# Row sums that go through DRAM in three units instead of one, with outputs scaled a pair later, and a third buffer for weight quarters

## The chip, the cores and the metric

The kernel runs on one core of one Trainium2 chip. The metric is device time in microseconds of one execution of the whole program. Three executions of the kernel before gave a median of 539.22 us (536.98 to 544.5). The engines are PE (TensorE, matrix products and transposes), DVE (VectorE), ACT (ScalarE), POOL (GpSimd) and SP (SyncE), whose queue issues nearly all DMAs of this program, strictly in the order in which they are written.

## The reference

Attention with a learned position bias for 4 batches, 8 heads, 576 positions and head size 64, followed by a gated feed-forward block (512 to 1024 to 512) with a convolution over three positions:

```python
scores = scale * q @ k.T + bias            # bias: a small network on the distance |i - j|
attn   = exp(scores - max) ; attn = attn / (sum(attn) + 1e-09)
x      = attn @ v                          # (4, 576, 512), heads side by side
h      = relu(x @ w_in)
out    = (h * sigmoid(conv3(h))) @ w_out
```

What matters for this change is the division by the sums of the rows. The kernel leaves it out of the attention matrix, computes the output of the pair unscaled, and multiplies it by the inverse sums afterwards. And the feed-forward weights, in float32, are split into two parts that TensorE multiplies at its faster float32 rate; this is done a quarter of 128 rows at a time, in small steps beside the attention.

## The kernel before

**Pairs and units.** Attention goes through 16 pairs (two heads, one batch), numbered n = 0 to 15, four batches for each pair of heads. A pair has five units, in the order `units = [1, 2, 3, 4, 0]`; `ui` is the place in this list, 0 to 4. I write (n, ui). In the loop over units (`for u, (n, t) in enumerate(flat)`), a unit does the scores of the unit two ahead (L341 on PE; L348 on DVE adds the bias and takes the minimum of the negated scores), the exponentials of the unit one ahead (L362, ACT), and its own transposes (L397, PE, copied out by ACT L88 and DVE L91) and products with v (L441, PE). The order on every engine is the order of the Python program: nothing is reordered, so an instruction that waits holds up all that stands behind it on its engine.

**The sums.** At the end of (n, 0) `invert(n - 1)` takes the reciprocals of the sums of pair n-1 (L461, L462, DVE). In (n, 2) they are transposed with the other blocks (L404) and copied to `rt` (L91). Then, still in (n, 2), `normalise(n - 1)` has SP store `rt` to DRAM in three small DMAs (`r_d<-rt`, L472 to L474) and read it back spread over 64 partitions each in two DMAs (`rb<-r_d`, L477, 144 KB each). The read waits on SP until the stores have landed. In (n, 4) `apply_norm(n - 1, rb)` has POOL multiply the output of the pair by `rb` (L483, 128 x 576). `rb` has one buffer.

**The weight quarters.** There are 28. Every second unit SP is asked for one (`raw_w`, L118, 256 KB); three units later its steps begin, in the two units that follow, one step per half unit: ACT L96 and DVE L97 (`w<-raw_w`), DVE L99, DVE L103, and in the fourth step POOL's split (L130, L131) of `w` into `wi` or `wo`. The tile `w` has one place for all quarters, so L97 of the next quarter, at the start of the next unit, waits for POOL's split of this one. `raw_w` has two buffers, and the ask for quarter j+2 stands in the unit in which L96 and L97 free the buffer of quarter j.

**SP's other work.** In (n, 2) it loads q and k of pair n+2 (L149, L150, four DMAs) and v of pair n+1 (L164 to L167, four DMAs). When the next pair of heads is near (from (n, 3) of pairs 2, 6 and 10 to (n, 2) of the pair behind) it also loads the bias rows of the next pair of heads, two DMAs per unit (L175, 288 KB each; L177).

After the loop come the last pair's sums and the feed-forward block (L504, L699 to L729).

Of the kernel before, what the change touches and what calls it, by code (L numbers as in the profile page):

```python
# [9 lines left out]
F32 = mybir.dt.float32  # L10
F32R = mybir.dt.float32r
I32 = mybir.dt.int32
# [7 lines left out]
def attention_ffn_kernel(  # L20
# [11 lines left out]
    nc = tc.nc  # L32
    B, S, DM = out.shape
# [5 lines left out]
    P = 128  # L39
# [19 lines left out]
    def pool(stack, name, bufs, **kw):  # L59
        return stack.enter_context(tc.tile_pool(name=name, bufs=bufs, reuse_waits="tile", **kw))  # L60
# [10 lines left out]
    e_p = pool(ctx, "e", 2)  # L71
    woe_p = pool(ctx, "woe", 1)
# [11 lines left out]
    NSEQ = len(seq)  # L84
# [32 lines left out]
    def load_w(raw, src):  # L117
        nc.sync.dma_start(raw.rearrange("p n t -> p (n t)"), src.bitcast(I32))  # L118
# [14 lines left out]
    with tc.manual_schedule():  # L133
# [9 lines left out]
        def load(n):  # L143
            p, b = seq[n]
            qks[n] = t = q_p.tile([P, KO + S], F32, name="qk")
            keys = qk[b, p, :, KO:].rearrange("d (h a s) -> d a h s", h=2, a=2)
            for a in range(2):
                rows = slice(D * a, D * a + D)
                nc.sync.dma_start(t[rows, 0:KO], qk[b, p, :, 0:KO])  # L149
                nc.sync.dma_start(halves(t[rows, KO:]), keys[:, a])  # L150
# [147 lines left out]
        rb_p = pool(att, "rb", 1)  # L298
# [9 lines left out]
        xb = {0: x0}  # L308
# [18 lines left out]
        def scores(n, t, h):  # L327
            p, b = seq[n]
            qt, bt = qks[n], biast[p, t]
            if h == 0:  # L330
                if n not in sms:
                    sms[n] = sm_p.tile([P, 9], F32, name="sm")
                nms[n, t] = sm_p.tile([P, 2], F32, name="nm")
                new_sp(n, t)
            ps = psS.tile([P, 2, 512], F32, name="s")
            ops = [(h, h * QW + P * t)] if t else [(1, QW), (0, 0)]

            for i, (hh, qo) in enumerate(ops):
                for a in range(2):
                    rows = slice(D * a, D * a + D)  # L340
                    nc.tensor.matmul(  # L341
                        ps[:, a, 0:HS],
                        qt[rows, qo:qo + P],
                        qt[rows, KO + hh * HS:KO + hh * HS + HS],
                        start=(i == 0),
                        stop=(i == len(ops) - 1),
                    )
            nc.vector.tensor_tensor_reduce(  # L348
                out=halves(spt[n, t][0][:, h]),
                in0=ps[:, :, 0:HS],  # L350
                in1=halves(bt[:, h]),
                op0=ALU.add,
                op1=ALU.min,
                scale=-scale,
                scalar=3.0e38,
                accum_out=nms[n, t][:, h:h + 1],
            )

        def expo(n, t, h):
            sp, nm = spt[n, t][0], nms[n, t]  # L360
            col = 4 * h + t - 1 if t else 8
            exps[n, t, h] = nc.scalar.activation(  # L362
                sp[:, h], sp[:, h], AF.Exp, bias=nm[:, h:h + 1], scale=-1.0,
                accum_out=sms[n][:, col:col + 1],
            )
# [6 lines left out]
        def ends_group(n, t):  # L372
            return t in (0, 2, 4) or n == 0 and t == 3
# [93 lines left out]
            rts[n] = r_p.tile([9, P], F32, name="rt")  # L467
            dve(rts[n], ps[0:9, 0:P])

        def normalise(n):  # L470
            rt = rts.pop(n)
            nc.sync.dma_start(r_d[n, 0, TL:].rearrange("(t x) -> t x", x=P), rt[0:4])  # L472
            nc.sync.dma_start(r_d[n, 1, TL:].rearrange("(t x) -> t x", x=P), rt[4:8])
            nc.sync.dma_start(r_d[n:n + 1, :, 0:TL], rt[8:9].rearrange("o (h x) -> o h x", h=2))  # L474
            rb = rb_p.tile([P, S], F32, name="rb")
            for h in range(2):
                nc.sync.dma_start(rb[D * h:D * h + D], r_d[n, h:h + 1, :].to_broadcast([D, S]))  # L477
            return rb

        def apply_norm(n, rb):  # L480
            p, b = seq[n]
            assert waiting[n] == 0
            nc.gpsimd.tensor_mul(xb[b][:, p], xb[b][:, p], rb)  # L483


        xss = {}
# [10 lines left out]
        def ffn_in(b, f):  # L497
            ps = psS.tile([P, 2, 512], F32, name="s")
            cs = slice(f * P, f * P + P)
            i = 0  # L500
            for c in range(KC):
                for pw, px in ((0, 0), (0, 1), (1, 0)):
                    for a in range(2):
                        nc.tensor.matmul(  # L504
                            ps[:, a, 0:HS],
                            wi[c][:, pw, cs],
                            xss[b, c][:, px, a * HS:(a + 1) * HS],
                            start=(i == 0),
                            stop=(i == 3 * KC - 1),
                        )  # L510
                    i += 1
            if (b, f) in ((0, 0), (0, 1)):
                h = e_p.tile([P, S], F32, name="h")
            else:
                h = g_p[0].tile([P, S], F32, name="h", tag="g")
            nc.scalar.activation(halves(h), ps[:, :, 0:HS], AF.Relu)  # L516
            return h
# [35 lines left out]
        def heads(t):  # L553
            return (0, 1) if t else (0,)
# [48 lines left out]
                for h in heads(flat[0][1]):  # L603
                    expo(*flat[0], h)
        pv_share = (2, 5, 3, 2, 3)
        rb = None
        hs_ff = {}
        raw_w = {}
        job_steps = iter(())
# [3 lines left out]
        for u, (n, t) in enumerate(flat):  # L613
            p, b = seq[n]
            ui = units.index(t)
            for h in range(2):
                if u + 2 < NU:
                    if h in heads(flat[u + 2][1]):
                        scores(*flat[u + 2], h)
                if u + 1 < NU and h in heads(flat[u + 1][1]):  # L620
                    expo(*flat[u + 1], h)
            transposes(n, t, 0)
            next(job_steps, None)

            parts = len(fill) if u < 5 else pv_share[ui]
            while fill and parts > 0:
                fill.popleft()()
                parts -= 1
            if t:
                transposes(n, t, 1, n - 1 if ui == 2 and n else None)  # L630
            next(job_steps, None)
            del spt[n, t]
            if u + 2 >= NU:
                f = u + 2 - NU
                hs_ff[0, f] = ffn_in(0, f)
            if u == 1 or n and ui == 2 and n + 2 < NSEQ:
                load(2 if u == 1 else n + 2)
            if u in conv_weights:
                conv_weights[u]()

            for at, do in ((u - 8, "load"), (u - 11, "split")):
                job = at // 2
                if at % 2 == 0 or not 0 <= job < 4 * KC + 2 * FE:
                    continue
                if job < 4 * KC:
                    src, dst = w_in[job // 4 * P:job // 4 * P + P], wi[job // 4]
                else:
                    src, dst = w_out[(job - 4 * KC) // 2 * P:(job - 4 * KC) // 2 * P + P], wo[(job - 4 * KC) // 2]
                cs = slice(job % 4 * 256, job % 4 * 256 + 256) if job < 4 * KC else slice(job % 2 * 256, job % 2 * 256 + 256)
                if do == "load":  # L650
                    raw_w[job] = e_p.tile([P, 256, 2], I32, name="raw_w", tag="h")
                    load_w(raw_w[job], src[:, cs])
                else:
                    job_steps = split_w_steps(e_p, dst[:, :, cs], raw_w.pop(job), ("cv", "cv"))
            if u + 2 < NU:
                n2, t2 = flat[u + 2]
                p2, b2 = seq[n2]
                if b2 == B - 1 and p2 + 1 < NP:
                    load_bias(p2 + 1, t2)
            if ui == (0 if n > 1 else 1) and n > 0:  # L660
                invert(n - 1)
            if ui == (2 if n > 1 else 3) and 1 <= n and n + 1 < NSEQ:
                load_v(n + 1)
            if ui == 2 and n > 0:
                rb = normalise(n - 1)
            if ends_group(n, t):
                fill.extend(pv_parts(n, group(n, t)))
            if ui == 4 and n > 0:
                apply_norm(n - 1, rb)
            if n == NSEQ - 2 and ui > 1:  # L670
                x_parts(0, ui - 2)
            if n == NSEQ - 1 and ui == 0:
                x_parts(0, 3)
            if n == NSEQ - 1 and ui in (1, 2):
                load_wo(FE - 1 + ui)
# [1 line left out]
            fill.popleft()()  # L677
        invert(NSEQ - 1)
        turn_sums(NSEQ - 1)
        apply_norm(NSEQ - 1, normalise(NSEQ - 1))  # L680
        att.close()


# [194 lines left out]
```

## Time and profile before

| | |
|---|---|
| median of three executions | 539.22 us (536.98 to 544.5) |
| the profiled execution | 545.77 us, of which the trace spans 543.9 us |
| PE busy | 503.7 us (93%) |
| DVE busy | 389.1 us (72%) |
| ACT busy | 313.5 us (58%) |
| POOL busy | 103.4 us (19%) |
| mean granted clock of TensorE | 0.971 |

How to read it: the attention loop lies between about 66 and 325 us of the span, the bias network before it and the feed-forward block behind it. PE is the engine that is nearly always busy, so time is lost where PE stands, and where its granted clock (1.00 is 2.4 GHz, 0.50 is 1.2 GHz) is low. In a row of a timeline the first number is the start in us from the span's start, the second the duration, and the brackets at the end give how long the engine stood idle just before, and what ended that wait.

### The profile page before, as it was taken

The page shows a single profiled execution, that of the slowest core. Times are in us where ns is not written, and L with a number is a line of the kernel's source. Part 1 is how long each engine was busy: PE and PEld are TensorE (multiplying, and loading weights), DVE is VectorE, ACT ScalarE, POOL GpSimd, SP SyncE. Part 2 cuts the span into 40 slices and gives each one's busy share as a digit, 9 for nine tenths or more (in the row PEclk, how much of TensorE's full clock was granted, in tenths as well). Part 3 has the DMA queues.
Part 4 walks back from the last instruction along what each step waited for, and adds up shares of the span by engine and source line. Part 5 has one row for each costly group of instructions (what it writes and reads, how often), then busy time and mean ns, then how long its engine had stood idle before and what let it go on. Part 6 is the DMA issues. An engine that isn't in the chain of part 4 may idle for free.

```text
span 543.9 us, 11908 instructions
## 1 busy us (share of the span) xinstructions
PE 503.7 (93%) x4542; PEld 389.3 (72%) x4542; DVE 389.1 (72%) x919; ACT 313.5 (58%) x813; POOL 103.4 (19%) x123
## 2 busy tenths in 40 slices
PE   5999989995899799898989999989999999999995
PEld 3332467774577577575767768978998899889985
DVE  6999677683788488586777763996499349928910
ACT  6888778784588477576767773662262235215510
POOL 1000001021222212232122541453007000700000
PEclk9999999999799899899999999979999999999998
DMA  6789545596557766557776211000200200020001
GB/s 164 265 245 342 205 114 129 126 281 165 141 126 184 233 185 160 137 145 217 190 190 158 66 57 62 23 0 0 78 2 1 78 20 0 1 78 0 2 39 60
DMA packets 32707, 63.50 MB, mean 117 GB/s; under 512 B 5490, under 2 KB 11146, under 8 KB 32650
## 3 DMA queue, kind: packets, MB, share of 16 engines
q1 hardware_dynamic: 32506, 62.66, 40.2%
q8 instruction: 36, 0.59, 0.5%
q14 instruction: 21, 0.17, 0.1%
q10 hardware_dynamic: 144, 0.08, 0.1%
HBM read 46.74 MB, written 15.98 MB: 115 GB/s over the span
## 4 chain that ended last, share of the span: by engine, by line
PE 58%; DMA 12%; DVE 5%; ACT 5%; POOL 3%; SPq 2%; issue 1%; POOLq 0%; DVEq 0%
PE s L504 16%; PE tp L729 14%; PE o L441 10%; PE s L341 7%; PE tp L397 6%; PE o L729 4%; DMA rb<-r_d 4%; DMA qk<-in_qk_dram 4%; DMA r_d<-rt 3%; ACT sp L362 2%; POOL x L483 2%; DVE cv L704 1%; ACT pt L88 1%; DMA bt<-bias_d 1%; ACT x L88 1%
## 5 line engine op out<-in xcount | busy, mean ns | idle before, releaser
L348 DVE CUSTOM_DVE_ANT_0 sp<-s,bt 128x576 f32<-128x576 f32 x144 | 103.6, 750 | 22.2 <-PE s L341 11.4
L362 ACT ACTIVATE sp<-sp,nm 128x576 f32<-128x576 f32 x144 | 109.9, 766 | 1.7 <-DVE nm L348 1.6
L441 PE MATMUL o<-pt,vt 128*64 128x256 f32 (+2 forms) x940 | 100.7, 344 | 10.1 <-DVE pt L91 7.7
L504 PE MATMUL s<-xs,wi 128*128 128x288 f32 x768 | 106.6, 301 | 2.7 <-ACT h L516 2.7
L504 PEld LDWEIGHTS s<-xs,wi 128*128 128x128 f32 x768 | 105.4, 193 | 3.7 <-ACT h L516 2.9
L397 PE MATMUL tp<-identr,sr 64*128 64x64 f32 x1312 | 97.0, 264 | 11.5 <-DVE rt L91 7.6
L397 PEld LDWEIGHTS tp<-identr,sr 64*128 64x128 f32 x1312 | 75.0, 138 | 44.5 <-issue 20.5
L341 PE MATMUL s<-qk 64*128 64x288 f32 x640 | 103.2, 437 | 0.7 <-DVE nm L348 0.6
L88 ACT ACTIVATE pt<-tp 128x256 f32<-128x256 f32 (+2 forms) x160 | 59.6, 383 | 63.1 <-PE tp L397 34.2
L91 DVE COPY pt<-tp 128x256 f32<-128x256 f32 (+2 forms) x160 | 66.5, 425 | 29.6 <-PE tp L397 15.7
L441 PEld LDWEIGHTS o<-pt,vt 128*64 128x64 f32 x940 | 53.2, 139 | 30.5 <-DVE pt L91 9.6
L341 PEld LDWEIGHTS s<-qk 64*128 64x128 f32 x640 | 59.7, 193 | 18.2 <-DVE pt L91 4.6
L729 PE MATMUL tp<-wo,g 128*128 128x512 f32 x288 | 70.2, 390 | 0.0
L704 DVE SCALAR_TENSOR_TENSOR cv<-h,cw,cv 128x575 f32<-128x575 f32 x64 | 60.8, 950 | 2.4 <-ACT cv L699 0.4
L483 POOL TENSOR_TENSOR x<-x,rb 128x576 f32<-128x576 f32 x16 | 22.8, 1425 | 206.5 <-ACT pt L88 101.6
L729 PEld LDWEIGHTS tp<-wo,g 128*128 128x128 f32 x288 | 54.0, 188 | 11.0
L260 PE MATMUL s<-y,pars 128*32 128x512 f32 (+8 forms) x352 | 46.4, 509 | 4.2 <-ACT st L286 2.0
L243 DVE TENSOR_SCALAR y<-tl,inv,nb 128x512 f32<-128x512 f32 (+8 forms) x116 | 49.9, 504 | 0.0
L516 ACT ACTIVATE h<-s 128x576 f32<-128x576 f32 x32 | 20.8, 650 | 48.9 <-PE s L504 48.8
L710 ACT ACTIVATE cv<-cv 128x576 f32<-128x576 f32 x32 | 21.8, 682 | 29.5 <-DVE cv L704 29.5
L260 PEld LDWEIGHTS s<-y,pars 128*32 128x32 f32 x352 | 16.1, 115 | 28.0 <-DVE y L243 13.3
L130 POOL TENSOR_SCALAR xs<-x 128x576 fp32r<-128x576 f32 x16 | 15.1, 942 | 83.5 <-PE s L504 83.5
(66 smaller groups left out, 454.5 us busy)
## 6 DMA issues: line engine op xcount, KB each, us to landing
qk<-in_qk_dram SPq DMA_DIRECT2D x32, 320.0 KB
bt<-bias_d SPq DMA_DIRECT2D x32, 288.0 KB
bias_d<-st SPq DMA_DIRECT2D x14, 607.0 KB
qk<-in_qk_dram SPq DMA_DIRECT2D x32, 144.0 KB
rb<-r_d SPq DMA_DIRECT2D x32, 144.0 KB
out_dram<-o SPq DMA_DIRECT2D x17, 256.0 KB
raw_w<-in_moe_w_in_dram SPq DMA_DIRECT2D x16, 256.0 KB
vt<-in_v_dram SPq DMA_DIRECT2D x16, 224.0 KB
```

The lines of the kernel that those rows point to most:

```text
L88: nc.scalar.activation(o, i, AF.Copy)
L91: nc.vector.tensor_copy(o, i)
L243: nc.vector.tensor_scalar(y, dist[:, 0:n], inv[:, ig:ig + 1], nb1, op0=ALU.mult, op1=ALU.max)
L260: nc.tensor.matmul(ps[32 * j:32 * j + 32, a // 512 if n > 512 else blk % 2, 0:min(n - a, 512)], w2b, ys[j][:, a:min(n, a + 512)], start=Tr ...
L341: nc.tensor.matmul(ps[:, a, 0:HS], qt[rows, qo:qo + P], qt[rows, KO + hh * HS:KO + hh * HS + HS], start=(i == 0), stop=(i == len(ops) - 1),)
L348: nc.vector.tensor_tensor_reduce(out=halves(spt[n, t][0][:, h]), in0=ps[:, :, 0:HS], in1=halves(bt[:, h]), op0=ALU.add, op1=ALU.min, scale ...
L362: exps[n, t, h] = nc.scalar.activation(sp[:, h], sp[:, h], AF.Exp, bias=nm[:, h:h + 1], scale=-1.0, accum_out=sms[n][:, col:col + 1],)
L397: tr = nc.tensor.transpose(ps[a][0:cols, bk - 4 * h].bitcast(F32R), spf[ra, j:j + cols], identr[ra, ra])
L441: nc.tensor.matmul(po[hs, oc], vt[:, slot, :], rhs, start=(c == 0), stop=(c == 4))
L504: nc.tensor.matmul(ps[:, a, 0:HS], wi[c][:, pw, cs], xss[b, c][:, px, a * HS:(a + 1) * HS], start=(i == 0), stop=(i == 3 * KC - 1),)
L704: nc.vector.scalar_tensor_tensor(out=cv[:, o:o + S - 1], in0=h[:, i:i + S - 1], scalar=cw[:, f, kk:kk + 1], in1=cv[:, o:o + S - 1], op0=AL ...
L729: nc.tensor.matmul(ps, lhs(f, gi), wo[f][:, wj, cs], start=(f == 0 and i == 0), stop=(f == FC - 1 and i == 2),)
```

## The change

The one function `normalise` becomes two. `store_sums(n - 1)` stands in (n, 3), a unit later than before; `spread_sums(n - 1)`, the read back, stands in (n, 4), two units later; `apply_norm(n - 2)` stands in (n, 1), which for the same pair is two units after its old place. `load_v` of (n, 2) thereby stands ahead of the stores, as it did before, but the read back has moved behind what stands in (n, 3). For the last pairs the calls follow after the loop. The weight quarters are asked for in the unit before (u - 7 in place of u - 8 in a test that takes every second unit, so an ask moves from odd u to the even u ahead of it), and every third of them takes its buffer from the pool `woe`, so there are three.

```diff
-        def normalise(n):
+        def store_sums(n):
             rt = rts.pop(n)
             nc.sync.dma_start(r_d[n, 0, TL:].rearrange("(t x) -> t x", x=P), rt[0:4])
             nc.sync.dma_start(r_d[n, 1, TL:].rearrange("(t x) -> t x", x=P), rt[4:8])
             nc.sync.dma_start(r_d[n:n + 1, :, 0:TL], rt[8:9].rearrange("o (h x) -> o h x", h=2))
-            rb = rb_p.tile([P, S], F32, name="rb")
+
+        def spread_sums(n):
+            rbs[n] = rb = rb_p.tile([P, S], F32, name="rb")
             for h in range(2):
                 nc.sync.dma_start(rb[D * h:D * h + D], r_d[n, h:h + 1, :].to_broadcast([D, S]))
-            return rb
 
-        def apply_norm(n, rb):
+        rbs = {}
+
+        def apply_norm(n):
             p, b = seq[n]
             assert waiting[n] == 0
-            nc.gpsimd.tensor_mul(xb[b][:, p], xb[b][:, p], rb)
+            nc.gpsimd.tensor_mul(xb[b][:, p], xb[b][:, p], rbs.pop(n))
...
-            for at, do in ((u - 8, "load"), (u - 11, "split")):
+            for at, do in ((u - 7, "load"), (u - 11, "split")):
...
-                    raw_w[job] = e_p.tile([P, 256, 2], I32, name="raw_w", tag="h")
+                    raw_w[job] = (e_p if job % 3 else woe_p).tile([P, 256, 2], I32, name="raw_w", tag="h")
                     load_w(raw_w[job], src[:, cs])
...
-            if ui == 2 and n > 0:
-                rb = normalise(n - 1)
+            if ui == 3 and n > 0:
+                store_sums(n - 1)
+            if ui == 4 and n > 0:
+                spread_sums(n - 1)
             if ends_group(n, t):
                 fill.extend(pv_parts(n, group(n, t)))
-            if ui == 4 and n > 0:
-                apply_norm(n - 1, rb)
+
+            if ui == 1 and n > 1:
+                apply_norm(n - 2)
...
         invert(NSEQ - 1)
         turn_sums(NSEQ - 1)
-        apply_norm(NSEQ - 1, normalise(NSEQ - 1))
+        apply_norm(NSEQ - 2)
+        store_sums(NSEQ - 1)
+        spread_sums(NSEQ - 1)
+        apply_norm(NSEQ - 1)
```

SP's queue in pair 6, from the last load of v to the bias rows. `raw_w` is a weight quarter, `r_d<-rt` a store of sums, `rb<-r_d` their read back, `bt` bias rows. Before:

```order
L167 DMA vt_107<-in_v_dram 64x64
L472 DMA r_d<-rt 4x128
L473 DMA r_d<-rt 4x128
L474 DMA r_d<-rt 2x1x64
L477 DMA rb<-r_d 64x576 x2
L175 DMA bt<-bias_d 128x576 x2
L118 DMA raw_w<-in_moe_w_in_dram 128x512
L175 DMA bt<-bias_d 128x576 x4
```

With the change:

```order
L167 DMA vt_107<-in_v_dram 64x64
L118 DMA raw_w<-in_moe_w_in_dram 128x512
L175 DMA bt<-bias_d 128x576 x2
L472 DMA r_d<-rt 4x128
L473 DMA r_d<-rt 4x128
L474 DMA r_d<-rt 2x1x64
L175 DMA bt<-bias_d 128x576 x2
L479 DMA rb<-r_d 64x576 x2
L118 DMA raw_w<-in_moe_w_in_dram 128x512
L175 DMA bt<-bias_d 128x576 x4
```

The read back, which stood right behind the stores, now has two bias DMAs between it and them, and a quarter and two more bias DMAs ahead of the stores.

POOL's queue from the multiply for pair 4 to the multiply for pair 5 (L483 before, L486 with the change), with the splits of weight quarters (L130, L131) behind them. Before:

```order
L483 TENSOR_TENSOR x_121<-x_121,rb 128x576
L130 TENSOR_SCALAR wi_758<-w 128x256
L131 TENSOR_TENSOR wi_758<-w,wi_758 128x256
L130 TENSOR_SCALAR wi_759<-w 128x256
L131 TENSOR_TENSOR wi_759<-w,wi_759 128x256
L483 TENSOR_TENSOR x_945<-x_945,rb 128x576
```

With the change:

```order
L486 TENSOR_TENSOR x_121<-x_121,rb 128x576
L130 TENSOR_SCALAR wi_759<-w 128x256
L131 TENSOR_TENSOR wi_759<-w,wi_759 128x256
L130 TENSOR_SCALAR wi_759<-w 128x256
L131 TENSOR_TENSOR wi_759<-w,wi_759 128x256
L486 TENSOR_TENSOR x_945<-x_945,rb 128x576
```

The multiply for pair 4 stood ahead of the last split into `wi_758`, and now stands behind it: one quarter, which is two units, further on.

## Rows read from the trace of the kernel before

**Rows 1.** Waits, 66 to 325 us: engine, line, releaser; total us, times, longest.

```profile
POOL x L483 <- DMA rb<-r_d: 80.0, 10, 16.0
DVE w L97 <- POOL wi L131: 17.7, 5, 7.7
DVE w L97 <- POOL wo L131: 8.4, 3, 4.0
PE o L441 <- DVE pt L91: 7.7, 3, 2.9
PE tp L397 <- DVE rt L91: 7.6, 3, 5.4
```

**Rows 2.** The same view for SP's queue, 66 to 325 us.

```profile
SPq L477 <- DMA r_d<-rt: 27.1, 17, 2.8
SPq L118 <- DVE w L97: 25.5, 7, 6.1
```

**Rows 3.** Timeline 178 to 187 us, one wait of PE followed back.

```profile
178.15 1.11 SPq L477 DMA_DIRECT2D rb<-r_d  x2
...
182.76 1.40 POOL L483 TENSOR_TENSOR x<-x,rb 128x576 f32<-128x576 f32 x1 [8.54 <-DMA rb<-r_d]
...
184.61 0.73 POOL L131 TENSOR_TENSOR wi<-w,wi 128x256 fp32r<-128x256 f32 x1
...
185.37 0.29 DVE L97 TENSOR_SCALAR w<-raw_w 128x256 int32<-128x256 int32 x1 [4.46 <-POOL wi L131]
...
186.12 1.12 PE L441 MATMUL o<-pt,vt 128*64 128x256 f32 x4 [2.89 <-DVE pt L91]
```

**Rows 4.** Stretch 186 to 189: busy PE, PEld, DVE, ACT, POOL; clock, DMA share, GB/s.

```profile
186.00:189.00 3.00, 2.88 (x13) 1.36 (x14) 1.74 (x6) 0.00 (x0) 1.09 (x2) 0.50 1.03 335
```

**Rows 5.** Timeline of DVE: the reciprocals at the ends of (n, 0).

```profile
124.10 0.22 DVE L462 RECIPROCAL rr<-rr 128x9 f32<-128x9 f32 x1
149.60 0.22 DVE L462 RECIPROCAL rr<-rr 128x9 f32<-128x9 f32 x1
164.32 0.22 DVE L462 RECIPROCAL rr<-rr 128x9 f32<-128x9 f32 x1
179.02 0.22 DVE L462 RECIPROCAL rr<-rr 128x9 f32<-128x9 f32 x1
200.55 0.21 DVE L462 RECIPROCAL rr<-rr 128x9 f32<-128x9 f32 x1
235.26 0.21 DVE L462 RECIPROCAL rr<-rr 128x9 f32<-128x9 f32 x1
250.09 0.21 DVE L462 RECIPROCAL rr<-rr 128x9 f32<-128x9 f32 x1
286.46 0.22 DVE L462 RECIPROCAL rr<-rr 128x9 f32<-128x9 f32 x1
302.52 0.22 DVE L462 RECIPROCAL rr<-rr 128x9 f32<-128x9 f32 x1
```

**Rows 6.** Timeline of DVE, a small wait for POOL's split.

```profile
289.99 0.29 DVE L97 TENSOR_SCALAR w<-raw_w 128x256 int32<-128x256 int32 x1 [1.62 <-POOL wo L131]
```

**Rows 7.** Timeline 104 to 138 us, SP and PE around pairs 2 to 4.

```profile
104.53 0.62 SPq L474 DMA_DIRECT2D r_d<-rt  x1
107.38 1.12 SPq L477 DMA_DIRECT2D rb<-r_d  x2
129.05 1.61 PE L441 MATMUL o<-pt,vt 128*64 128x256 f32 x12 [1.65 <-DMA vt<-in_v_dram]
137.69 0.69 PE L397 MATMUL tp<-identr,sr 64*128 64x64 f32 x7 [5.35 <-DVE rt L91]
```

**Rows 8.** Timeline 230 to 238 us, a multiply beside DVE's L103.

```profile
231.05 0.41 DVE L103 SCALAR_TENSOR_TENSOR w<-u,w 128x256 int32<-128x256 int32 x1
...
236.48 1.41 POOL L483 TENSOR_TENSOR x<-x,rb 128x576 f32<-128x576 f32 x1 [3.71 <-ACT sr L323]
237.03 1.15 DVE L103 SCALAR_TENSOR_TENSOR w<-u,w 128x256 int32<-128x256 int32 x1
```

More of the change, by code (lines that the diff above doesn't have):

```diff
@@ L605, in attention_ffn_kernel @@
         pv_share = (2, 5, 3, 2, 3)
-        rb = None
         hs_ff = {}
```

## The prediction

> **What bounds the kernel now.** The page gives PE busy for 93% of the span, so I look for the places where PE stands, and for what ends these waits. First the list of waits in the attention loop [rows 1]. PE's large waits there are for copies by DVE: 7.7 us in three times and 7.6 us in three times. DVE itself waits, in its line L97 (the first step of a weight quarter), for POOL's split of the quarter before: 17.7 us in five times and 8.4 us in three times, 26.1 us together, the longest 7.7 us. And POOL waits for the sums read back from DRAM: 80.0 us in ten times. POOL has time to wait; DVE, which stands behind it, has not.
>
> Then the timeline of one case, read from its end [rows 3]. PE gets its copy at 186.12 after 2.89 us of idleness; DVE's L97, which stands ahead of that copy, came at 185.37 after 4.46 us; POOL's split began its last part at 184.61, straight behind the multiply, which came at 182.76 because `rb` landed only then. SP had asked for `rb` at 178.15. So a transfer that PE needs for nothing stops PE, through two queues that keep their order. It costs more than the wait: in the 3 us behind it PE's granted clock is 0.50, which is 1.2 GHz [rows 4]. PE had stood for 2.89 us before.
>
> What one such case costs in all, clock included, is best read from a mark that comes once in every pair, the reciprocals [rows 5]. From 149.60 to 164.32 to 179.02 nothing of the kind costs time, and a pair takes 14.72 and 14.70 us, so 14.71 us, or 2.94 us a unit. From 179.02 to 200.55 (the case above) it takes 21.53 us: 6.82 us more, of which 2.89 are the wait and some 3.9 the low clock. From 124.10 to 302.52 lie ten pairs in 178.42 us. Ten plain ones would be 147.1 us. So 31.3 us of the loop are lost to waits of this kind and their clock.
>
> **The change, part by part.** It adds and removes no instruction: 16 multiplies, 48 stores, 32 reads and 28 quarters stay. It moves them.
>
> *The multiply two units on.* L97 of DVE must not wait for a multiply that waits for `rb`. The multiply moves two units, hence the L97 that stands behind it too: `rb` may land 2 x 2.94 = 5.88 us later than before. The eight waits of L97 are the measure of how late it was. The next longest after the one of 7.7 us is that of the case above, 4.46 us [rows 3]; seven go, with at least 1.4 us to spare, if `rb` does not come later. The eighth was 7.7 us [rows 1] and would keep 1.8 us.
>
> *The read back, later on SP.* What the ask is now behind must be subtracted. An ask takes SP about 0.56 us (1.12 us for two [rows 7]). In a plain pair one or two quarters come ahead of the ask in place of standing behind it, 0.6 to 1.1 us; on the other side SP spends 27.1 us in 17 times waiting at the read for the stores to land, 1.6 us each [rows 2], and the quarter between stores and read, where there is one, fills part of that. I take 0.5 us net: the spare stays near 0.9 us. In pairs 6 and 10 four bias DMAs also come ahead. Their asks are 4 x 0.56 = 2.2 us, mostly inside SP's wait for the stores; their 1152 KB at the 335 GB/s of [rows 4] are 3.4 us of transfer. At 178.15 the stores' landing had left the transfer engines little to do, so I charge about half of it: 1.3 to 1.7 us against the 1.4 us to spare. L97 may wait there for up to about a microsecond. Wait sizes have a price: 1.62 us [rows 6] stand in a pair of 302.52 - 286.46 = 16.06 us, 1.35 us over the plain one. I put two such places at 0.7 us each. Lower bound nothing, upper bound the full case, 6.82 us each.
>
> *The wait of 7.7 us, pairs 3 and 4.* Here the queue of SP was late from pair 2 on: it had stood from 105.15 to 107.38 for the stores [rows 7], with bias DMAs behind it. These now stand ahead of the read, so up to 2.2 us of the delay of all that follows goes, less two asks for quarters, 1.1 us. 7.7 - 2.2 + 1.1 = 6.6 us against 5.88 leaves about 0.7 us, at a price of some 0.6 us. The wait of PE for v at 129.05, 1.65 us [rows 7], comes from the same late queue, and I let it go too. Its bounds are nothing and 1.65 us.
>
> *The weight quarters.* SP waited 25.5 us in seven times until DVE's L97 freed a buffer [rows 2]. With the third buffer the ask stands a unit after that step in place of beside it, so SP no longer stops there. By itself this is no time of PE's: nobody but SP waited. It keeps the q, k and v behind it from being late, and I price it at nothing. Were the cover gone, L96 and L97 would wait for the quarter itself, but it is asked for a unit earlier, 2.94 us, so this can only shrink.
>
> *After the loop.* The last multiplies stand behind PE's last transposes as before; nothing there is priced.
>
> The sum, in the profiled execution's own time: 545.77 - 31.3 + 1.4 + 0.6 = 516.5 us. It lies 6.55 us above the median of 539.22. Three executions spread over 7.5 us, while plain pairs repeat within 0.1 us [rows 5], so I believe that most of that difference lies in these waits and goes with them; 1.5 us of it I take as a fixed difference. **Forecast: 515 us.**
>
> **Rivals.**
>
> *The bias pairs keep their waits.* In pairs 2, 6 and 10 the read back is behind four more DMAs of 288 KB. For it: those bytes are real, and the spare of 1.4 us is small. Against: SP's stop for the stores, which they fill. If all three cost the full 6.82 us, 20.5 us come back: about 535 us, which would be no difference of 2%. Chance 0.12.
>
> *Multiply and DVE hinder each other.* Before, eight of the multiplies had DVE standing behind them; now they all run while it works. Beside the multiply of 236.48 the step L103 took 1.15 us where the one of 231.05 took 0.41 [rows 8]: 0.74 us. Were that on the path in all twelve pairs with quarters, 8.9 us: about 524 us. The Trainium skill, "SBUF — State Buffer", section "Who interferes with whom", has it as a rule: a DVE instruction with two inputs in SBUF contends with a GpSimd instruction that reads SBUF, and the second waits until the first is finished. By that rule, and with nothing to cover it, it is this rival that holds, and the row agrees with the rule as far as the duration of L103 goes. Against it as a cost: that pair, 235.26 to 250.09, took 14.83 us [rows 5], 0.12 us above the plain one, so DVE's slack covers it. Chance 0.07.
>
> *Slower.* `rb` has one buffer. The read for pair n-1, in (n, 4), may be asked for only when the multiply for pair n-2, in (n, 1), is done. A late multiply so makes SP stand, with the next pair's weights, q, k and v behind it, and the next multiply late in turn: a wait in every pair in place of eight. Ten pairs at 6.82 us are 68 us, less 31.3: 545.77 + 36.9, about 583 us. It decides from the point where a multiply is over three units late, 8.8 us. Against: from ask to multiply were 4.6 us (178.15 to 182.76) and the multiply 1.40 us [rows 3], 6 us in a cycle of 14.71, so a delay heals within a pair. Chance 0.04.
>
> **How the numbers follow.** The forecast's case has 0.72, the three rivals 0.23, and 0.05 I leave for what I do not see. 2% of the median, about what a measurement of this kernel can tell from no change, puts the bounds at 528.4 and 550.0 us. The forecast's case, the DVE rival and a third of the bias rival lie below 528.4: 0.87. Within 2% lie the rest of the bias rival and a little of the unknown: 0.09. Slower: 0.04. The range begins at 539.22 - 31.3 = 508 us, which is the case that the 6.55 us are all a fixed difference and no wait is left, and goes to 529 us, which takes in the DVE rival and two full waits that stay (515 - 2.0 + 13.6 = 527).
>
> **What will show it.** In the changed kernel's list of waits L97's wait for POOL's splits should fall from 26.1 us to under 4, PE's two waits for DVE's copies from 15.3 us to under 3, SP's wait for L97 to near nothing. POOL may still wait for `rb`: that is no fault. The reciprocals should be 14.7 us apart in at least eight of ten pairs, and the granted clock 1.00 through the loop. If these waits are gone and the pairs are still longer than 15 us, the price of the wait was wrong and something else in the unit bounds it; if L97 still waits in pairs 3, 7 or 11, the bias DMAs are the reason; if SP waits at the read for POOL, the single buffer is.

## The result, and the profile after

| | before | after |
|---|---|---|
| median (runs) | 540.44 us (4) | 518.62 us (4) |
| lowest to highest | 536.98 to 544.5 | 517.68 to 520.76 |
| profiled execution, span | 545.77, 543.9 us | 517.68, 515.8 us |
| mean granted clock | 0.971 | 0.992 |

The ratio is 0.9599 [0.9522, 0.9676]: faster, 3.6 us above the forecast of 515 and inside the range. Between the two profiled executions lie 28.1 us, between the medians 21.8: the profiled execution of the kernel before was 5 us over its median. The ratios, here and below, leave out executions more than 1.5% above the fastest of the same kernel, which are three of the ten of R alone, whose median of 549.25 us stands beside a ratio of 1.0088 for this reason.

The list of waits of the changed kernel, 66 to 300 us (its loop ends earlier), answers to [rows 1].

```profile
POOL x L486 <- DMA rb<-r_d: 39.2, 7, 16.1
PE tp L397 <- DVE rt L91: 0.7, 1, 0.7
DVE w L97 <- POOL wo L131: 0.7, 1, 0.7
```

L97's waits for POOL fell from 26.1 us to 0.7, PE's two waits for DVE's copies from 15.3 to 0.7. POOL still waits for `rb` seven times, and nobody pays. The same view of SP's queue answers to [rows 2]; SP's wait for L97 to free a buffer, 25.5 us before, is not in it any more.

```profile
SPq L479 <- DMA r_d<-rt: 15.8, 17, 1.9
```

The timeline of the changed kernel around its tightest place, the counterpart of [rows 3].

```profile
169.62 1.13 SPq L479 DMA_DIRECT2D rb<-r_d  x2
...
174.85 1.41 POOL L486 TENSOR_TENSOR x<-x,rb 128x576 f32<-128x576 f32 x1 [4.98 <-DMA rb<-r_d]
...
176.71 0.74 POOL L131 TENSOR_TENSOR wi<-w,wi 128x256 fp32r<-128x256 f32 x1
...
177.53 0.27 DVE L97 TENSOR_SCALAR w<-raw_w 128x256 int32<-128x256 int32 x1
```

The multiply waits for `rb` as before, 5.2 us after the ask. But L97 behind it has no bracket: the split ended at 177.45, and L97 began at 177.53 without waiting. The spare here is under 0.1 us; it is the read back that stands behind four bias DMAs.

The stretch of the ten pairs, and the 3 us of [rows 4], in the changed kernel (columns as in [rows 4], with the number of instructions behind each busy time):

```profile
124.20:274.89 150.69, 149.10 (x1848) 111.50 (x1844) 131.23 (x395) 121.31 (x376) 42.75 (x60) 1.00 0.77 194
186.00:189.00 3.00, 2.90 (x35) 2.55 (x37) 2.45 (x9) 2.52 (x10) 1.14 (x2) 1.00 0.50 129
```

The same 1848 matmuls as before in 150.69 us in place of 178.42: 27.73 of the 28.1 us between the profiled executions lie in these ten pairs. The granted clock is 1.00 throughout.

The mark of [rows 5], DVE's reciprocals, and beside it a mark on PE, the products of one block at the end of each pair; both of the changed kernel, over the same two pairs.

```profile
184.71 0.22 DVE L462 RECIPROCAL rr<-rr 128x9 f32<-128x9 f32 x1
184.96 0.80 PE L441 MATMUL o<-pt,vt 128*64 128x64 f32 x20
199.40 0.22 DVE L462 RECIPROCAL rr<-rr 128x9 f32<-128x9 f32 x1
199.98 0.80 PE L441 MATMUL o<-pt,vt 128*64 128x64 f32 x20
214.76 0.22 DVE L462 RECIPROCAL rr<-rr 128x9 f32<-128x9 f32 x1
215.01 0.80 PE L441 MATMUL o<-pt,vt 128*64 128x64 f32 x20
```

DVE's mark gives 14.69 and 15.36 us, PE's 15.02 and 15.03. By PE's mark nine of the ten pairs take 15.01 to 15.04 us, and the first, from 124.45 to 139.89, takes 15.44. The plain pair is 15.03 us, not 14.71.

### The profile page after: what moved, and what is told of

Its sections match the earlier page's. It is cut to its first block, busy times and chain, and to the rows that moved or that the text cites. A ratio compares the mean times of both kernels' runs of the same rounds, so it can differ in the third digit from the quotient of the medians.

```text
span 515.8 us, 11903 instructions
## 1 busy us (share of the span) xinstructions
PE 490.8 (95%) x4542; PEld 381.7 (74%) x4542; DVE 392.7 (76%) x919; ACT 313.5 (61%) x813; POOL 103.0 (20%) x123
## 4 chain that ended last, share of the span: by engine, by line
PE 67%; ACT 7%; DVE 5%; DMA 4%; SPq 1%; issue 1%; DVEq 0%
PE s L507 17%; PE tp L737 15%; PE o L441 12%; PE s L341 11%; PE tp L397 8%; PE o L737 4%; ACT sp L362 4%; DMA vt<-in_v_dram 2%; ACT pt L88 2%; DVE cv L712 2%; ACT x L88 1%; DMA bt<-bias_d 1%; DVE cv L719 1%; DVE sp L348 1%; DVE w L103 1%
## 5 line engine op out<-in xcount | busy, mean ns | idle before, releaser
L507 PE MATMUL s<-xs,wi 128*128 128x288 f32 x768 | 105.5, 299 | 2.7 <-ACT h L519 2.7
L507 PEld LDWEIGHTS s<-xs,wi 128*128 128x128 f32 x768 | 104.3, 191 | 3.7 <-ACT h L519 2.9
L341 PE MATMUL s<-qk 64*128 64x288 f32 x640 | 100.8, 428 | 1.0 <-DVE nm L348 0.9
L397 PEld LDWEIGHTS tp<-identr,sr 64*128 64x128 f32 x1312 | 73.5, 136 | 34.7 <-issue 18.5
L397 PE MATMUL tp<-identr,sr 64*128 64x64 f32 x1312 | 94.3, 260 | 4.6 <-ACT pt L88 3.8
L441 PE MATMUL o<-pt,vt 128*64 128x256 f32 (+2 forms) x940 | 93.9, 335 | 0.7 <-ACT x L88 0.7
L341 PEld LDWEIGHTS s<-qk 64*128 64x128 f32 x640 | 58.1, 188 | 18.4 <-DVE pt L91 4.2
L441 PEld LDWEIGHTS o<-pt,vt 128*64 128x64 f32 x940 | 50.4, 136 | 18.4 <-ACT x L88 1.2
L486 POOL TENSOR_TENSOR x<-x,rb 128x576 f32<-128x576 f32 x16 | 23.1, 1444 | 167.0 <-ACT sr L323 92.3
L718 ACT ACTIVATE cv<-cv 128x576 f32<-128x576 f32 x32 | 21.8, 682 | 28.7 <-DVE cv L712 28.7
L130 POOL TENSOR_SCALAR xs<-x 128x576 fp32r<-128x576 f32 x16 | 14.7, 917 | 83.2 <-PE s L507 83.2
```

The source lines that it names most:

```text
L341: nc.tensor.matmul(ps[:, a, 0:HS], qt[rows, qo:qo + P], qt[rows, KO + hh * HS:KO + hh * HS + HS], start=(i == 0), stop=(i == len(ops) - 1),)
L397: tr = nc.tensor.transpose(ps[a][0:cols, bk - 4 * h].bitcast(F32R), spf[ra, j:j + cols], identr[ra, ra])
L441: nc.tensor.matmul(po[hs, oc], vt[:, slot, :], rhs, start=(c == 0), stop=(c == 4))
L507: nc.tensor.matmul(ps[:, a, 0:HS], wi[c][:, pw, cs], xss[b, c][:, px, a * HS:(a + 1) * HS], start=(i == 0), stop=(i == 3 * KC - 1),)
```

## Experiments

The change has three parts that can be made apart: the multiply two units on (M), store and read back later (R), the quarters asked for sooner with a third buffer (W). All eight combinations ran. Ratios are against the kernel before, run beside each set of experiments (medians 541.78, 540.82 and 540.13; 540.44 for the change).

| | median us | ratio |
|---|---|---|
| none (before) | 540.44 | 1 |
| M | 540.18 | 0.9974 [0.9933, 1.0014] |
| R | 549.25 | 1.0088 [1.0039, 1.0137] |
| W | 543.2 | 1.0034 [0.9997, 1.0071] |
| R, W | 541.04 | 1.0014 [0.9977, 1.005] |
| M, W | 524.96 | 0.9715 [0.9654, 0.9777] |
| M, R | 519.88 | 0.9592 [0.9526, 0.9658] |
| M, R, W (the change) | 518.62 | 0.9599 [0.9522, 0.9676] |

**M and R, quarters as before.** Against the changed kernel:

```diff
-            for at, do in ((u - 7, "load"), (u - 11, "split")):
+            for at, do in ((u - 8, "load"), (u - 11, "split")):
...
-                    raw_w[job] = (e_p if job % 3 else woe_p).tile([P, 256, 2], I32, name="raw_w", tag="h")
+                    raw_w[job] = e_p.tile([P, 256, 2], I32, name="raw_w", tag="h")
```

> The sums' part of the change alone: stores in (n, 3), read back in (n, 4), multiply two units on; weight quarters as before (two buffers, asked for at u - 8). Theory (what cost time was that L97 of DVE stood behind POOL's split, behind a multiply that waited for rb): 517 to 521 us, the waits of L97 for POOL's splits under 4 us; SP may still stop for a buffer, for nobody's loss. Rival (the early weight quarters are part of it, since SP's stops for L97 made rb and v late): 525 us or more, with waits of L97 left in pairs 3, 7 or 11.

519.88 us (518.95 to 522.44). Nearly the whole gain comes without W. The timeline at the place shown above tells what W is worth there:

```profile
170.74 1.13 SPq L479 DMA_DIRECT2D rb<-r_d  x2
...
178.29 1.41 POOL L486 TENSOR_TENSOR x<-x,rb 128x576 f32<-128x576 f32 x1 [8.18 <-DMA rb<-r_d]
...
180.91 0.29 DVE L97 TENSOR_SCALAR w<-raw_w 128x256 int32<-128x256 int32 x1 [3.07 <-POOL wi L131]
```

`rb` was asked for 1.1 us later and took 7.6 us to let the multiply begin, not 5.2. L97 waits 3.07 us, and that pair takes 17.22 us on PE in place of 15.03. So the bias pairs' rival is real at one place in three once W is away, and what the expectation called nobody's loss is 2.2 us of PE's there. The medians differ by 1.3 us, from different sets of runs; the intervals of the ratios overlap, so W's worth behind M and R is not told from nothing by the times.

**W alone.** Against the kernel before, the two lines of the diff above the other way round.

> The weights' part alone: third buffer, quarters asked for at u - 7; sums and multiply as before. Theory: 533 to 541 us, since rb lands where it did and the multiply stands where it did; SP's 25.5 us of waits for L97 go, L97's 26.1 us of waits for the splits stay above 18. Rival (SP's stops made rb late): under 528 us, with L97's waits under 12 us.

543.2 us (541.49 to 547.87), just above the expected range. L97 still waits 24.9 us for the splits (16.5 in five times, 8.4 in three). The quarters were not the first thing late.

**M alone.** Against the kernel before (the calls after the loop follow in the same way):

```diff
             if ui == 2 and n > 0:
-                rb = normalise(n - 1)
+                store_sums(n - 1)
+                spread_sums(n - 1)
...
-            if ui == 4 and n > 0:
-                apply_norm(n - 1, rb)
+            if ui == 1 and n > 1:
+                apply_norm(n - 2)
```

> Only the multiply is moved two units on; stores and read back stay in (n, 2), weight quarters as before. Theory (the place of the multiply in POOL's queue is all of the gain, the later places on SP's queue give nothing): 517 to 521 us. Rival (the read must not stand straight behind the stores, since SP's stop for their landing delays all behind it): 523 us or more, with waits of PE for v or of L97 left in pairs 3 and 4.

540.18 us (536.5 to 544.48): no gain, and here my theory fell. The waits for the splits are gone as it says; others stand in their place. The timeline's rows of the weight steps that wait, and of PE behind the first of them:

```profile
138.44 0.44 ACT L96 ACTIVATE u<-raw_w 128x256 f32<-128x256 f32 x1 [9.95 <-DMA raw_w<-in_moe_w_in_dram]
138.48 0.29 DVE L97 TENSOR_SCALAR w<-raw_w 128x256 int32<-128x256 int32 x1 [8.62 <-DMA raw_w<-in_moe_w_in_dram]
139.50 0.69 PE L397 MATMUL tp<-identr,sr 64*128 64x64 f32 x7 [6.54 <-DVE rt L91]
...
207.09 0.29 DVE L97 TENSOR_SCALAR w<-raw_w 128x256 int32<-128x256 int32 x1 [4.57 <-DMA raw_w<-in_moe_w_in_dram]
...
273.82 0.29 DVE L97 TENSOR_SCALAR w<-raw_w 128x256 int32<-128x256 int32 x1 [5.85 <-DMA raw_w<-in_moe_w_out_dram]
```

L97 now waits for the quarter itself, in pairs 4, 8 and 12, behind the bias rows. These three pairs take 28.16, 21.00 and 23.07 us on PE, every other one between 124.50 and 301.98 takes 15.02 to 15.09. In the same three pairs PE also waits for v, 4.7 us together, so their loss is not the quarter's alone. The clock takes its part as before: in the 6 us behind the first, the granted clock is 0.50.

```profile
140.00:146.00 6.00, 6.00 (x43) 3.85 (x43) 4.19 (x12) 2.96 (x11) 1.13 (x2) 0.50 0.52 127
```

Why the quarter is late, SP's queue in this kernel shows, the asks of the first case:

```profile
128.29 0.61 SPq L474 DMA_DIRECT2D r_d<-rt  x1
130.08 1.12 SPq L479 DMA_DIRECT2D rb<-r_d  x2
131.31 1.00 SPq L118 DMA_DIRECT2D raw_w<-in_moe_w_in_dram  x2
```

The ask for the quarter stands behind the read back, and the read back behind the landing of the stores. In the first place it could have been seen. In the trace of the kernel **before**, at the wait of 7.7 us of [rows 1], ACT's step of the same quarter stands 1.9 us ahead of L97's:

```profile
134.90 0.44 ACT L96 ACTIVATE u<-raw_w 128x256 f32<-128x256 f32 x1 [6.55 <-DMA raw_w<-in_moe_w_in_dram]
...
136.82 0.29 DVE L97 TENSOR_SCALAR w<-raw_w 128x256 int32<-128x256 int32 x1 [7.70 <-POOL wi L131]
```

L97 needs that quarter too. It was put down to POOL, which came last, but the quarter had landed only some 1.9 us before it. Without POOL about 5.8 of the 7.7 us would have stayed. By the same reading 1.2 of the 2.75 us of L97's wait at 277.07 in pair 12 would have stayed. In pair 8 the trace before did not show it: ACT's step had its quarter without a wait there.

```profile
204.70 0.47 ACT L96 ACTIVATE u<-raw_w 128x256 f32<-128x256 f32 x1
...
205.95 0.29 DVE L97 TENSOR_SCALAR w<-raw_w 128x256 int32<-128x256 int32 x1 [1.11 <-POOL wi L131]
```

With M alone that pair begins 3.0 us earlier on PE (197.80 against 200.81), because pair 7 no longer loses its time, while SP asks for the quarter 2.4 us later (203.15 against 200.75). Why the asks come later there was not followed up. So the second wait is in part hidden behind the first one, and in part made by its removal.

**R alone.** Against the changed kernel, the multiply back in (n, 4) and the quarters as before:

```diff
-            if ui == 1 and n > 1:
-                apply_norm(n - 2)
+            if ui == 4 and n > 0:
+                apply_norm(n - 1)
```

> Only stores and read back are moved, to (n, 3) and (n, 4); the multiply stays in (n, 4), weight quarters as before. Theory: a later place in SP's queue is not a later time, only as many asks later as now stand ahead (0.6 to 1.1 us in plain pairs, some 2 us in pairs 2, 6 and 10), so the ten waits grow a little: 543 to 556 us. Rival (two units on the queue are two units of time, 5.9 us): each of ten pairs loses at least 5 us more, 585 us or more.

549.25 us (542.07 to 552.03), inside the expected range: with a read two units later and the multiply left where it was, the first wait is a little larger (L97 27.7 us against 26.1, 17.6 in six times and 10.1 in four; the longest 8.4). It does not set off the runaway of 585 us and more.

**The landing of `rb` taken away.** Does the rest of the time in M alone come from `rb` in some other way? This kernel multiplies the outputs by themselves, so that POOL never waits for the sums; the division by the sums is left out of the result. Stores and reads stay in their old places.

```diff
-            nc.gpsimd.tensor_mul(xb[b][:, p], xb[b][:, p], rb)
+            nc.gpsimd.tensor_mul(xb[b][:, p], xb[b][:, p], xb[b][:, p])
```

> The kernel before, with the multiply's second operand no longer rb but the output itself (it squares the outputs of a pair in place of scaling them); stores, read back and weight quarters are issued as before, and the multiply stands where it did. So the multiply has all its work and place, but no landing to wait for. Theory: 516 to 520 us, about the changed kernel, L97's waits for POOL's splits under 2 us. Rival (the multiply itself, 1.4 us of POOL beside DVE, costs time by where it stands): 525 us or more.

536.64 us (534.09 to 539.76), ratio 0.9932 [0.9897, 0.9968]. That misses by over 16 us: with no wait for `rb` at all the kernel is hardly faster. The time lies where the rival had it, but its cause is not the rival's either: L97 has no wait for a split left, and waits for the quarter instead. The rows of L97 that wait, and SP's queue at the first:

```profile
133.07 0.29 DVE L97 TENSOR_SCALAR w<-raw_w 128x256 int32<-128x256 int32 x1 [4.83 <-DMA raw_w<-in_moe_w_in_dram]
...
199.61 0.29 DVE L97 TENSOR_SCALAR w<-raw_w 128x256 int32<-128x256 int32 x1 [4.97 <-DMA raw_w<-in_moe_w_in_dram]
...
267.61 0.29 DVE L97 TENSOR_SCALAR w<-raw_w 128x256 int32<-128x256 int32 x1 [5.73 <-DMA raw_w<-in_moe_w_out_dram]
```

```profile
127.50 1.12 SPq L477 DMA_DIRECT2D rb<-r_d  x2
128.72 1.00 SPq L118 DMA_DIRECT2D raw_w<-in_moe_w_in_dram  x2
```

The same three places as with M alone, so the second wait does not depend on how the first one is removed. The quarter is asked for at 128.72. By the order of the program the same quarter is asked for at 115.79 in the changed kernel, a unit sooner and with a buffer free, and at 123.36 in M and R, where the ask stands ahead of the stores:

```profile
115.79 0.53 SPq L118 DMA_DIRECT2D raw_w<-in_moe_w_in_dram  x1
122.89 0.27 SPq L472 DMA_DIRECT2D r_d<-rt  x1
```

```profile
123.36 0.34 SPq L118 DMA_DIRECT2D raw_w<-in_moe_w_in_dram  x1
123.79 0.29 SPq L472 DMA_DIRECT2D r_d<-rt  x1
```

(first the changed kernel, then M and R). So R and W do the same for the quarter by different means: each brings its ask ahead of SP's stop for the stores. The next three runs test that.

**M and W.** M alone, with the quarters of the change.

> Multiply two units on and early weight quarters with the third buffer; stores and read back stay in (n, 2). New theory (two transfers were late at the pairs behind the bias rows, rb and the weight quarter, and each alone is enough to stop DVE; either the early quarters or the later read cures the second): 518 to 525 us, waits of L97 and L96 under 3 us together, PE's waits for v, up to 5 us, may stay. Rival (the later read is needed by itself): 530 us or more. The first theory (only rb) cannot tell this from the multiply alone and would say 540.

524.96 us (523.28 to 527.96): W, worth nothing by itself, is worth 15 us when M is there. On DVE no wait for a quarter is left, and 1.1 us for splits; ACT's L96 waits once for a quarter, 1.9 us, so L97 and L96 together come to the 3 us that were expected at most. What is left against the change, 6.3 us between the medians and 8.9 between the profiled executions, goes with PE's waits for v in the same three pairs, 6.2 us where up to 5 were expected (timeline):

```profile
128.69 1.58 PE L441 MATMUL o<-pt,vt 128*64 128x256 f32 x12 [1.05 <-DMA vt<-in_v_dram]
193.27 2.90 PE L441 MATMUL o<-pt,vt 128*64 128x256 f32 x12 [4.19 <-DMA vt<-in_v_dram]
256.88 1.58 PE L441 MATMUL o<-pt,vt 128*64 128x256 f32 x12 [0.96 <-DMA vt<-in_v_dram]
```

The pairs with them take 16.23, 21.61 and 16.33 us, 9.1 us over plain ones. In the second case eight bias DMAs stand on SP between the read back and the next q, k and v; in the changed kernel four, the others being ahead of the read. The last DMA of v is issued at 188.45 here and at 183.13 there:

```profile
188.45 0.47 SPq L167 DMA_DIRECT2D vt<-in_v_dram  x1
```

```profile
183.13 0.47 SPq L167 DMA_DIRECT2D vt<-in_v_dram  x1
```

That, as the order of the queue has it, is what R does beyond W; no run moves the bias DMAs alone.

**No landing, and W.** The multiply of the output by itself, with the quarters of the change (the division is left out as above).

> As the run without a landing to wait for (the multiply squares the outputs in place of scaling them, at its old place), now with the third buffer and the early quarters. New theory: both late transfers are gone, 517 to 523 us, no wait of L97 or L96 over 1 us. Rival (DVE's waits for the quarters at 133, 200 and 268 us were not what made that run slow): 530 us or more.

523.54 us (521.08 to 524.36), half a microsecond above the expected range. Again only waits for v are left: 0.67, 3.48 and 0.63 us. The landing of `rb` and the landing of the quarter, both taken off the path, give what M and W give.

**R and W, the multiply left.** The changed kernel with the multiply back in (n, 4), as in R alone.

> Stores in (n, 3), read back in (n, 4), early quarters with the third buffer; the multiply stays in (n, 4). New theory: the quarters are in time, but rb is as late for the multiply as before or later, and L97 waits for POOL's splits in eight or more places: 540 to 552 us. Rival (with SP relieved, rb comes in time for the old place): under 530 us.

541.04 us (538.13 to 544.47): without M nothing is gained, since L97 keeps 25.3 us of waits for the splits (17.5 in four times, 7.8 in three, where eight places or more were expected).

**The multiply one unit earlier than in the change.** Against the changed kernel:

```diff
-            if ui == 1 and n > 1:
+            if ui == 0 and n > 1:
                 apply_norm(n - 2)
```

> The changed kernel with the multiply in (n, 0) in place of (n, 1), one unit earlier. For pairs where the multiply now falls on the other side of a split, L97 has two units less to spare, for the others nothing changes. By the changed kernel's trace rb of pairs 2, 6 and 10 landed at 132.0, 191.3 and 252.2 us, and with 2.6 us of POOL's work L97 of (4, 2), (8, 2) and (12, 2) would be late by 6.2, 5.0 and 5.8 us, while rb of the other pairs lands in time. Theory: three waits of L97, 14 to 18 us together, each with 2 to 4 us of low clock: 534 to 545 us. Rival (the spare was large, and one unit of the two would have done): 518 to 522 us.

538.2 us (533.3 to 542.41), ratio 0.993 [0.9889, 0.9972]. The waits come back in the three pairs behind the bias rows:

```profile
134.52 0.29 DVE L97 TENSOR_SCALAR w<-raw_w 128x256 int32<-128x256 int32 x1 [6.12 <-POOL wi L131]
...
201.54 0.29 DVE L97 TENSOR_SCALAR w<-raw_w 128x256 int32<-128x256 int32 x1 [4.83 <-POOL wi L131]
...
270.15 0.29 DVE L97 TENSOR_SCALAR w<-raw_w 128x256 int32<-128x256 int32 x1 [6.43 <-POOL wo L131]
```

In the first case `rb` lets the multiply begin at 131.91, in the changed kernel at 132.00; but here the last split of a quarter, and so the next L97, stands behind it, and in the changed kernel that split stands ahead of it and was done at 127.74. A quarter comes in every second unit, so the slack that one unit gives is that of two. These pairs take 23.22, 21.95 and 22.40 us on PE, 6.9 to 8.2 us over the plain pair, near the price that the prediction took from [rows 5].

**Two buffers, asked for a unit sooner.** Against the changed kernel:

```diff
-                    raw_w[job] = (e_p if job % 3 else woe_p).tile([P, 256, 2], I32, name="raw_w", tag="h")
+                    raw_w[job] = e_p.tile([P, 256, 2], I32, name="raw_w", tag="h")
```

> The changed kernel with two buffers for weight quarters, still asked for at u - 7. The ask now stands a unit ahead of the L97 that frees its buffer, so SP stops there for up to 2.9 us per quarter, and the stores, reads and loads behind it come later. Theory (rb of pair 5 lands with next to nothing to spare in the changed kernel, so later asks bring waits of L97 back in a few pairs): 521 to 532 us. Rival (SP has room enough): 517 to 520 us.

525.29 us (524.09 to 526.48), ratio 0.9714 [0.966, 0.9768]; 5.4 us slower than with neither half of W. The waits of SP's queue say why:

```profile
SPq L118 <- DVE w L97: 26.8, 16, 4.4
```

Asked for sooner without a buffer, SP stops at nearly every ask until L97 frees one, and what is behind it is late: L97 waits 3.26 and 2.11 us for splits again, PE 3.0 us for v. W's two halves belong together.

## Why the prediction was right, and what was wrong in it

**The forecast held** because the read back and the quarters moved together with the multiply. The reasoning for it, that the multiply's 5.88 us of slack are what removes the waits, is shown to be only half: M is necessary (R, W, and both gain nothing without it) but alone gains nothing either. The parts that it priced at a small loss or at nothing brought the other half; as far as the reasoning goes, that is luck.

**The step that failed: "By itself this is no time of PE's: nobody but SP waited ... and I price it at nothing."** And with it the 0.5 us net for the read's new place. At L97 two transfers are late, one behind the other: `rb`, through POOL, and the quarter. A wait list names the one that ends last. Take it away, and the program runs on into the other, and into v behind that: three pairs in M alone are 13.1, 6.0 and 8.0 us over the plain one, which is nearly the gain. W is worth 15 us behind M, R 20 us, and both together only 1 us more than R. The prediction had the case as the loss of a cover ("L96 and L97 would wait for the quarter itself") but said that it "can only shrink", which is right for the whole change and hid that this shrinking was needed.

**The wait of 7.7 us.** "2.2 us of the delay ... goes, less two asks": its working looked at POOL's queue alone. The row of 134.90, shown with M alone, says that most of that wait was the quarter's too.

**The mis-sized term: the plain pair.** 14.71 us was read between marks on DVE. The first of them was itself late: the instruction ahead of the reciprocal of 149.60 took 0.82 us beside the multiply of 148.13, and its counterpart a pair on 0.16. Rows of the kernel before:

```profile
148.13 1.41 POOL L483 TENSOR_TENSOR x<-x,rb 128x576 f32<-128x576 f32 x1 [6.70 <-DMA rb<-r_d]
```

```profile
148.75 0.82 DVE L461 TENSOR_SCALAR rr<-sm 128x9 f32<-128x9 f32 x1
...
164.13 0.16 DVE L461 TENSOR_SCALAR rr<-sm 128x9 f32<-128x9 f32 x1
```

DVE was late at 149.60 by some 0.66 us; on time, the first of the two pairs would have read about 15.4 us. The second, 14.70, had both its marks on time, and is short because the mark moves against PE: in the rows of the changed kernel above it stands 0.25, 0.58 and 0.25 us ahead of PE's, and from 169.93 to 230.04 four pairs in a row read 14.78, 14.69, 15.36 and 15.28, which are 60.11 us or four times 15.03. With 15.03 us, ten pairs are 150.3, the waits cost 178.42 - 150.3 = 28.1 us in place of 31.3, and 545.77 - 28.1 = 517.7 us; 517.68 was measured. The case of [rows 3] costs 6.2 us by PE's mark (179.61 to 200.81), not 6.82. The miss of 3.6 us against the median is made up of these 3.2, of 1.5 and 0.9 for the fixed difference below, less the residual of 2.0 that did not come: errors that in part cancel.

**The residual** of 2.0 us for bias pairs did not appear: L97's one wait is 0.7 us, and no pair of the ten lost time to it. But its spare is under 0.1 us in the second bias pair, and 3.07 us were missing there without W.

**The fixed difference** of 1.5 us between profiled execution and median did not appear either: 517.68 profiled, 518.62 the median. That the spread of the kernel before lies in these waits agrees with the runs, 7.5 us before and 3.1 after, but was not tested by itself.

**The rivals.** Slower by the single `rb` buffer: the read back waited for POOL for 0.3 us at the longest. The bias pairs kept nothing in the changed kernel; M alone shows that they are the right places, with the quarter and v late there in place of `rb`. Multiply and DVE hinder each other: they do, at a twentieth of the price. Timeline of the changed kernel in its one longer pair:

```profile
132.00 1.42 POOL L486 TENSOR_TENSOR x<-x,rb 128x576 f32<-128x576 f32 x1 [4.25 <-DMA rb<-r_d]
132.38 1.32 DVE L103 SCALAR_TENSOR_TENSOR w<-u,w 128x256 int32<-128x256 int32 x1
133.62 0.48 DVE L91 COPY pt<-tp 128x320 f32<-128x320 f32 x1
...
134.15 1.05 PEld L441 LDWEIGHTS o<-pt,vt 128*64 128x64 f32 x10 [0.22 <-DVE pt L91]
```

Beside the multiply L103 takes 1.32 us against the 0.41 of [rows 8], the copy behind it comes late, PE's weight load waits 0.22 us for that copy, and the pair takes 15.44 us; I put its 0.41 us down to this, untested. Two more L103, of 0.96 us at 233.90 and 0.89 at 253.01, stand beside multiplies in pairs of 15.04 and 15.03 us and cost nothing. So the rule of the Trainium skill ("SBUF — State Buffer", "Who interferes with whom") agrees with the durations: each of the three, and the one of [rows 8], ends 0.28 or 0.29 us after its multiply does. As time of the kernel it is 0.4 us in ten pairs, where the rival had 8.9 in twelve.

**What was to show it.** L97's wait under 4 (0.7), PE's under 3 (0.7), SP's wait for L97 gone, clock 1.00 in the loop: as said. The reciprocals 14.7 us apart: wrong, by the mark. Pairs over 15 us were to mean that the price of the wait was wrong: they take 15.03, and the price was too high by the mis-sized pair.

**A sum.** The cases that the prediction names as below 528.4 us come to 0.83 (0.72, 0.07 and a third of 0.12); its 0.87 holds 0.04 of the unseen that it does not name.

## What to carry to other kernels

A wait names only the releaser that came last, so before pricing its removal look for another operand of the waiting instruction, or a neighbour that needs the same one (here ACT's L96), and see when that landed: the gain ends there at the latest. That would have shown two of the three places here; the third came up only when the time lost ahead of it was gone, which a run of the part alone showed. Parts that are worth nothing alone can be worth everything together, so a change that removes one of two waits is not disproved until the other is gone too. Measure a period on the engine that bounds the loop: PE's products gave 15.03 us in nearly every pair, DVE's reciprocals 14.69 to 15.36.

## What the runs showed of the hardware

A one-input instruction of DVE was lengthened beside POOL too: L461, 128x9, took 0.82 us beside a multiply in place of 0.16 (148.75, above), and ended 0.03 us after it. In the changed kernel it took 0.75 and 0.74 us beside POOL's L131, at 169.15 and 229.26. With M alone a wait of 6.54 us on PE left the granted clock at 0.50, which is 1.2 GHz, for at least the 6 us shown; after the 3.07 us wait of L97 in M and R the clock stayed at 1.00:

```profile
184.00:187.00 3.00, 3.00 (x40) 2.10 (x36) 2.78 (x10) 2.49 (x8) 1.14 (x2) 1.00 0.85 207
```

PE itself had stood for 1.54 us there, and that pair lost 2.19 us, not the 6.2 of the case of [rows 3], where PE had stood for 2.89.
